# Two attention and two gated-MLP layers on one core: another layout and pacing of the gate/up weight loads, with three smaller edits and new instruction orders

## The chip, the cores and the metric

The kernel runs on one core of one Trainium2 chip. The metric is device time in microseconds (us) for one execution; lower is better. The time of a kernel is the median of its runs, and a profile is one further execution, taken with the hardware profiler.

## What is computed

The input is x, one sequence of 2048 tokens by 448 features in bf16. Four layers follow each other, A, B, A, B, with the same weights for both A and both B, and each adds its result to x:

```python
x = x + _A_ref(_layernorm(x, axis=-1), A_wqkv, A_wo)
x = x + _B_ref(_layernorm(x, axis=-1), B_w_gate, B_w_up, B_w_down)
x = x + _A_ref(_layernorm(x, axis=-1), A_wqkv, A_wo)
x = x + _B_ref(_layernorm(x, axis=-1), B_w_gate, B_w_up, B_w_down)
```

A is attention with 16 heads of 28 features: each token attends to 8 tokens, itself and those 2, 4, ... 14 places before it. B is a gated MLP without a nonlinearity: `(x @ w_gate) * (x @ w_up)`, 1792 wide, then `@ w_down`.

## The kernel before

**Tiling.** Tokens live on partitions in 16 blocks of 128 (`x_sb`); even and odd tokens are stored in separate halves so that the stride of 2 becomes a stride of 1. Each layer runs in chunks of 256 or 512 tokens, and chunks of neighbouring layers interleave in the order of `SEQ` (A00 A01 B10 A02 B11 ...: A, layer 0, chunk 0, and so on). A chunk's rows are normalised on DVE and ACT (L724 to L745) and transposed, in layer 0 by PE with a copy out of PSUM by ACT or DVE (L755 and `ft`, L761), in later layers by a DMA transpose from SP (L748). An A chunk then makes queries and keys (`qk_chunk`, copies at L846) and values (`v_group`), scores (L958), exponentials (L965), masks (L975), the weighted sum (L995), normalisation, and the output product (`y_blocks`). A B chunk (`b_chunk`) has 14 gate/up units of 128 of the 1792 columns. Each unit is seven pairs of matmuls, gate and up side by side: a matmul here uses 64 of PE's 128 rows, so two that use different row halves run at once (helper `pair`, recorded as L489). ACT copies gate out (L1086), DVE multiplies by up (L1089), and the down products follow (L489, and L1101 at the end).

**Weights.** `WGU` holds gate and up for `b_chunk`. Before the change, partitions 0 to 63 hold gate and 64 to 127 hold up, for seven slabs k of 64 weight rows. Eight transfers fill it, one for each quarter of the columns of each matrix, each into 64 partitions with rows of 448 columns (896 bytes); a gate/up unit waits only for the quarters up to its own columns. The four `wo` transfers and the four `WD` transfers come after them, each `WD` transfer only when the one before has landed. The query/key weights arrive in `stage` in four row groups c (they take the space of `hT`), and are spread out into `WQK` by eight copies at L664: for each c one copy of all queries and one of all keys. Small constants go to a DRAM scratch tensor (`vones`), from which DMA transposes later bring part of the values (`vt_load`, L866) after copies out of `qk` (L855).

**Order.** Nothing is ordered by the chip alone. `Sched` collects operations and numbers them as they are added. `ORD` lists, for each of PE, ACT, DVE, POOL and SP, the numbers in the order in which that engine issues them. The estimates in the code (`lat`, `LINE_T` and others) only decide which PSUM banks are handed out and were used to find the lists. In `emit` each operation first waits for the semaphores of all that it depends on, and what follows on the same engine waits behind it. So a DMA on SP that waits for an earlier landing holds up every later DMA of SP. In SP's list of before, numbers 0 to 13 are the head loads, 78 is `vones`, 79 to 86 are gate/up, 87 to 90 `wo`, 91 to 93 the first three `WD`, and then come 291 and 293, the two DMA transposes that the first gate/up chunk (layer 1, chunk 0, 256 tokens) needs.

**Head loads.** SP and ACT issue the loads of x and of the query, key and value weights in the first microseconds. All of x is in five more transfers after the first block; chunk ("x", -1, 4) is the one that brings blocks 4 to 7, ("x", -1, 8) and ("x", -1, 12) the next ones.

Of the kernel before, what the change touches and what calls it, by code (L numbers as in the profile page):

```python
# [4 lines left out]
ACT = mybir.ActivationFunctionType  # L5
# [43 lines left out]
VONES_L = 13300.0  # L49
GUL = (14800.0, 1150.0)  # L50
WOL = 24300.0
# [12 lines left out]
}  # L64
SEQ = "A00 A01 B10 A02 B11 A03 A04 B12 A20 B13 A21 B14 B30 A22 B31 A23 B32 B33 B34".split()

# [1165 lines left out]
```

## Time and profile before

| | before |
|---|---|
| median of 3 runs | 391.69 us (390.35 to 392.07) |
| profiled execution, its own time | 392.11 us |
| its span, first to last instruction | 390.4 us |
| PE busy | 381.7 us, 98% of the span |
| PE weight loads busy | 217.5 us, 56% |
| DVE busy | 281.6 us, 72% |
| ACT busy | 192.7 us, 49% |
| POOL busy | 9.8 us, 3% |
| DMA | 22.49 MB in 56608 packets |
| mean granted TensorE clock | 0.996 |

The span is the time from the first to the last instruction of the program; the execution's own time is 1.7 us longer. A busy PE is not a PE at its peak: matmuls overlap, and a busy stretch may hold a slower clock. The granted clock is the share of full speed that the chip allows TensorE. A line number such as L489 can be that of a helper that makes many instructions, so groups are told apart by tiles as well: `ps<-xnTb,WGU` are gate/up matmuls, `ps<-xnTa,WQK` are queries and keys. The part "idle before" of a group names what ended the engine's waiting; "issue" means that the engine waited for nothing that the profile shows.

### The profile page before, as it was taken

How to read it: one execution, taken by the hardware profiler on the slowest of the kernel's cores; microseconds unless marked ns; L12 is line 12 of the kernel's file. 1: busy time of each engine (PE TensorE's matmuls, PEld its weight loads, DVE VectorE, ACT ScalarE, POOL GpSimd, SP SyncE). 2: the span in 40 equal slices, each digit the busy share in tenths (PEclk: the TensorE clock that was granted, in tenths of full speed). 3: DMA queues.
4: the chain of work that ended last, by engine and by line, in shares of the span. 5: the costliest groups of instructions: out<-in, count | busy, mean ns of one | idle time of the engine just before them, and what ended most of it. 6: DMA issues, size and time to landing. Idle time of an engine off the chain costs nothing.

```text
span 390.4 us, 14264 instructions
## 1 busy us (share of the span) xinstructions
PE 381.7 (98%) x6356; PEld 217.5 (56%) x6356; DVE 281.6 (72%) x609; ACT 192.7 (49%) x380; POOL 9.8 (3%) x41
## 2 busy tenths in 40 slices
PE   7979999999999999999999999999999999999997
PEld 3545558654454545544556678544555555555875
DVE  6967899898988578495667978667687688355423
ACT  4876897563724754065662436453354553033310
POOL 7020000000000000000000000000000000000000
PEclk9989999999999999999999999999999999999999
DMA  8994131900342001420402134130107002304002
GB/s 272 248 205 110 33 69 25 136 11 2 57 79 29 13 14 27 86 44 2 59 17 30 29 63 84 31 55 0 26 5 93 12 0 44 77 2 107 2 25 84
DMA packets 56608, 22.49 MB, mean 58 GB/s; under 512 B 44948, under 2 KB 56548, under 8 KB 56548
## 3 DMA queue, kind: packets, MB, share of 16 engines
q1 hardware_dynamic: 56116, 21.07, 28.0%
q8 instruction: 50, 0.82, 0.9%
q10 hardware_dynamic: 432, 0.52, 0.4%
q14 instruction: 10, 0.08, 0.1%
HBM read 8.54 MB, written 2.71 MB: 29 GB/s over the span
## 4 chain that ended last, share of the span: by engine, by line
PE 94%; DVE 2%; DMA 1%; ACT 1%; issue 1%; ACTq 0%; DVEq 0%
PE ps L489 86%; PE ps L958 3%; PE ps L995 2%; PE ps L492 1%; PE ps L1101 1%; DMA hT<-in_A_wqkv_dram 1%; ACT qk L846 0%; PE ps L755 0%; DVE xn_sb L745 0%; DVE oT L1033 0%; DVE qk L846 0%; DVE hT L1089 0%; ACT R_sb L1021 0%; DVE v_sb L938 0%; ACT O_sb L1006 0%
## 5 line engine op out<-in xcount | busy, mean ns | idle before, releaser
L489 PE MATMUL ps<-xnTb,WGU 64*128 64x512 bf16 (+1 forms) x1938 | 177.0, 333 | 0.0
L489 PEld LDWEIGHTS ps<-xnTb,WGU 64*128 64x128 bf16 x1938 | 97.1, 94 | 68.5 <-issue 1.2
L1086 ACT ACTIVATE g_sb<-ps 128x512 bf16<-128x512 f32 (+1 forms) x140 | 68.9, 510 | 106.3 <-PE ps L489 96.7
L1089 DVE TENSOR_TENSOR hT<-g_sb,ps 128x512 bf16<-128x512 bf16 (+1 forms) x140 | 77.1, 574 | 44.1 <-ACT g_sb L1086 39.4
L489 PE MATMUL ps<-WD,hT 64*128 64x448 bf16 x820 | 84.2, 349 | 0.8 <-DVE hT L1089 0.8
L489 PEld LDWEIGHTS ps<-WD,hT 64*128 64x128 bf16 x820 | 41.0, 94 | 34.1 <-issue 1.1
L489 PE MATMUL ps<-xnTa,WQK 64*128 64x512 bf16 (+1 forms) x500 | 53.6, 359 | 1.1 <-issue 0.7
L1050 DVE TENSOR_TENSOR x_sb<-x_sb,ps 128x448 bf16<-128x448 bf16 x62 | 36.8, 614 | 23.8 <-PE ps L489 23.8
L965 ACT ACTIVATE E_sb<-ps 128x1024 bf16<-128x1024 f32 (+1 forms) x36 | 33.7, 980 | 14.7 <-PE ps L958 14.3
L724 DVE BATCH_NORM_STATS2 st<-x_sb 128x6 f32<-128x448 bf16 x64 | 38.5, 615 | 1.5 <-DMA x_sb<-in_A_x_dram 1.3
L489 PEld LDWEIGHTS ps<-xnTa,WQK 64*128 64x128 bf16 x500 | 23.8, 96 | 24.5 <-issue 1.7
L745 DVE TENSOR_SCALAR xn_sb<-x_sb,mv,rstd 128x896 bf16<-128x896 bf16 (+1 forms) x64 | 36.0, 579 | 1.2 <-ACT rstd L729 1.0
L1021 ACT ACTIVATE R_sb<-R_sb 128x480 f32<-128x480 f32 (+1 forms) x34 | 20.1, 601 | 25.4 <-DVE R_sb L1020 25.3
L975 DVE TENSOR_TENSOR E_sb<-E_sb,MK 128x1024 bf16<-128x1024 bf16 (+2 forms) x40 | 23.9, 611 | 10.9 <-ACT E_sb L965 10.4
L846 ACT ACTIVATE qk<-ps 128x1024 bf16<-128x1024 f32 (+1 forms) x25 | 22.5, 918 | 17.3 <-PE ps L489 17.1
L489 PE MATMUL ps<-wo_g,oT 64*128 64x448 bf16 x252 | 29.1, 350 | 0.1
L1020 DVE STREAM_SHUFFLE R_sb<-O_sb 128x480 f32<-128x480 f32 (+1 forms) x34 | 22.9, 692 | 0.0
L1033 DVE TENSOR_TENSOR oT<-O_sb,R_sb 128x480 bf16<-128x480 f32 (+3 forms) x36 | 22.1, 625 | 0.9 <-ACT R_sb L1022 0.7
L489 PE MATMUL ps<-WV,xnTa 64*128 64x336 bf16 (+3 forms) x248 | 22.4, 304 | 0.1
L1022 ACT ACTIVATE R_sb<-R_sb 128x480 f32<-128x480 f32 (+1 forms) x34 | 19.9, 601 | 0.2
L489 PEld LDWEIGHTS ps<-wo_g,oT 64*128 64x128 bf16 x252 | 12.3, 94 | 11.0 <-DVE oT L1033 0.5
L846 DVE CAST qk<-ps 128x1024 bf16<-128x1024 f32 (+1 forms) x11 | 12.4, 1123 | 6.6 <-PE ps L489 6.6
(59 smaller groups left out, 192.5 us busy)
## 6 DMA issues: line engine op xcount, KB each, us to landing
out_dram<-x_sb SPq DMA_DIRECT2D x15, 112.0 KB, 1.8
WGU<-in_B_w_gate_dram SPq DMA_DIRECT2D x4, 392.0 KB, 8.8
WGU<-in_B_w_up_dram SPq DMA_DIRECT2D x4, 392.0 KB, 9.6
x_sb<-in_A_x_dram SPq DMA_DIRECT2D x3, 448.0 KB, 5.9
WD<-in_B_w_down_dram SPq DMA_DIRECT2D x2, 448.0 KB, 3.7
WD<-in_B_w_down_dram SPq DMA_DIRECT2D x2, 336.0 KB, 3.9
vt<-qk SPq DMA_DIRECT2D x42, 16.0 KB
xnTb<-xn_sb SPq DMA_TRANSPOSE x32, 3.1
```

The source lines that it names most:

```text
L489: return lambda E: E.matmul(out(), lhs(), rhs(), start=start, stop=stop)
L724: sc.add("dve", one(lambda E, B=B: E.bn_stats(st6[:, B, :], x_sb[:, B, :]), ("bn", li, B)), 525.0, deps=[("x", li - 1, B)] + ([("xn", li - ...
L745: sc.add("dve", one(lambda E, B=B, dst=dst, src=src: E.tensor_scalar(dst, src, mv[:, B, 0:1], rstd[:, B:B + 1], ALU.subtract, ALU.mult), ( ...
L846: return E.activation(dst, src, ACT.Copy) if hasattr(E, "activation") else E.tensor_copy(dst, src)
L965: return E.activation(E_sb[:, slot, 2 * hp:2 * hp + 2, 0:w], ps[:, b0:b0 + 2, 0:w], ACT.Exp, scale=SCALE)
L975: return E.tensor_tensor(e, e, m, ALU.mult)
L1020: sc.add("dve", one(lambda E: E.stream_shuffle(R_sb[:, rs, 0:w], O_sb[:, os_, 0:w], [DH] * 32), ("Rs", li, qb)), dve_est(w) + 100.0, deps= ...
L1021: sc.add("act", one(lambda E: E.activation(R_sb[:, rs, 0:w], R_sb[:, rs, 0:w], ACT.Ln), ("Rl", li, qb)), act_est(w, False), deps=[("Rs", l ...
L1033: return E.tensor_tensor(oT[:, :, a % HALF:a % HALF + z - a], O[:, :, a - tok:z - tok], R_sb[:, rs, 0:w].rearrange("p (h n) -> p h n", h=4 ...
L1050: sc.add("dve", one(lambda E: E.tensor_tensor(x_sb[:, B, :], x_sb[:, B, :], ps[:, bk[w], 0:D], ALU.add), ("x", li, B)), dve_est(D), deps=[ ...
L1086: sc.add("act", one(lambda E, gs=gs, bk=bk: E.activation(g_sb[:, gs, 0:nt], ps[:, bk[0], 0:nt], ACT.Copy), ("G", li, j, fc)), act_est(nt), ...
L1089: sc.add("dve", one(lambda E, gs=gs, bk=bk, fc=fc: E.tensor_tensor(hT[:, fc, hs, 0:nt], g_sb[:, gs, 0:nt], ps[:, bk[1], 0:nt], ALU.mult), ...
```

## The change

- **Gate/up layout and loads.** For gate, slab k keeps its 64 weight rows, but the first half of the columns (896) goes to partitions 0 to 63 and the second half to 64 to 127. For up, partitions 0 to 63 take the second half of the columns of slab k, and partitions 64 to 127 the first half of the columns of slab k+1 (of slab 0 for the last). So for each unit gate and up still lie in different partition halves: in units 0 to 6 gate is in the lower and up in the upper half, in units 7 to 13 the other way round, and the matmul pairs are written accordingly. There are 15 transfers in place of 8: seven for gate, six for up, and two of 64 partitions for up's remainder. Thirteen of them have 128 destination partitions, rows of 896 columns (1792 bytes), and a source pattern of three dimensions, `[2, 64, 896]`.
- **Waits.** A unit waits for all 15 transfers, not for the quarters up to its own.
- **Pacing.** `link` adds a transfer to a chain: it waits until the third-last one before it has landed. The chain begins with three loads of x; the 15 gate/up transfers, `vones` and the four `WD` transfers follow. The `wo` transfers now come before all of them.
- **Query/key copies.** Each of the eight copies at L664 takes half of the heads, of queries and keys together. In layer 0's first two chunks the units c = 0 and 1 wait for the first halves only.
- **Transposes.** In layer 0's first chunk the copy out of PSUM is made in two halves, which may go to different engines.
- **Orders.** All five lists in `ORD` are new. The numbering moves: 78 to 81 are `wo`, 82 to 96 gate/up, 97 `vones`, 98 to 101 `WD`, and most later numbers are higher by 9. SP's list begins 0, 1, 4 to 13, 78 to 98 in one run, then 583 (one copy out of `qk`), 302 and 300 (the two DMA transposes for the first gate/up chunk, formerly 293 and 291), then 509 and further copies.

```diff
-VONES_L = 13300.0
-GUL = (14800.0, 1150.0)
-WOL = 24300.0
+GUL = 2900.0
+DEPTH = 3
+WOL = 14000.0
...
-                src = stage[:, 2 * D * c + D * w:2 * D * c + D * (w + 1)].rearrange("p (h e) -> p h e", e=DH)
-                dst = WQK[:, c, w, :].rearrange("p (h e) -> p h e", e=32)[:, :, 0:DH]
+                src = stage[:, 2 * D * c:2 * D * (c + 1)].rearrange("p (w h e) -> p w h e", w=2, e=DH)[:, :, 8 * w:8 * w + 8, :]
+                dst = WQK[:, c, :, 256 * w:256 * w + 256].rearrange("p w (h e) -> p w h e", e=32)[:, :, :, 0:DH]
...
-    head_dma("sp", ones_dst, ones_src, ("vones",), "d_one", VONES_L, deps=["c_ones"])
-    for n in range(4):
-        f0, f1 = F // 4 * n, F // 4 * (n + 1)
-        for w, W_ in enumerate((B_w_gate, B_w_up)):
-            head_dma("sp", WGU[64 * w:64 * w + 64, :, f0:f1], W_[:, f0:f1].rearrange("(k p) f -> p k f", p=64), (("wg", "wu")[w], n), f"d_w{'gu'[w]}{n}", GUL[0] + GUL[1] * (2 * n + w))
...
-    prev = ("wo", 3)
+    chain = [("x", -1, 4), ("x", -1, 8), ("x", -1, 12)]
+
+    def link(dst, src, key, sem, lat, deps=()):
+        plain_dma("sp", dst, src, key, sem, deps=[chain[-DEPTH], *deps], lat=lat)
+        chain.append(key)
+
+    for w, W_ in enumerate((B_w_gate, B_w_up)):
+        for k in range(7):
+            v = W_[64 * k:64 * k + 64, :]
+            r = v.ap[0][0]
+            dst = WGU[:, k, w * F // 2:(w + 1) * F // 2]
+            if w == 0 or k < 6:
+                src = bass.AP(tensor=v.tensor, offset=v.offset + w * F // 2, ap=[[F // 2 if w == 0 else 64 * r - F // 2, 2], [r, 64], [1, F // 2]])
+                link(dst, src, (("wg", "wu")[w], k), f"d_w{'gu'[w]}{k}", GUL)
+            else:
+                link(dst[0:64], v[:, F // 2:F], ("wu", 6), "d_wu6", GUL)
+                link(dst[64:128], W_[0:64, 0:F // 2], ("wu", 7), "d_wu7", GUL)
+    link(ones_dst, ones_src, ("vones",), "d_one", WDL, ["c_ones"])
     for n in range(4):
         f0, f1 = (0, 4, 7, 11, 14)[n:n + 2]
-        plain_dma("sp", WD[:, f0:f1, :], B_w_down[128 * f0:128 * f1, :].rearrange("(c p) e -> p c e", p=128), ("wd", n), f"d_wd{n}", deps=[prev], lat=WDL)
-        prev = ("wd", n)
+        link(WD[:, f0:f1, :], B_w_down[128 * f0:128 * f1, :].rearrange("(c p) e -> p c e", p=128), ("wd", n), f"d_wd{n}", WDL)
...
-            return dict(bk=bk, out=out, lhs=lhs, rhs=rhs, n=n, kind="QKps", deps=WQK0 if (li, j) in NOPW else WQKR, keys=(("Kps", li, j, c), ("Qps", li, j, c)), c=c)
+            return dict(bk=bk, out=out, lhs=lhs, rhs=rhs, n=n, kind="QKps", deps=WQK0 if (li, j) in NOPW and c > 1 else WQK0[::2] if (li, j) in NOPW else WQKR, keys=(("Kps", li, j, c), ("Qps", li, j, c)), c=c)
...
-            return dict(bk=acq, out=out, n=nt, deps=[(w, n) for w in ("wg", "wu") for n in range((128 * fc + 127) // (F // 4) + 1)],
+            return dict(bk=acq, out=out, n=nt, deps=[(w, k) for w in ("wg", "wu") for k in range(7 + (w == "wu"))], row=(64 * r, 64 - 64 * r), col=(col, F // 2 + col),
                         keys=(("Gps", li, j, fc), ("Ups", li, j, fc)), fc=fc)
```

More of the change, by code (lines that the diff above doesn't have):

```diff
@@ L137 @@
     LINE = 256
-    LINE_T = ((75000.0, 4300.0), (24000.0, 5000.0), (11000.0, 6500.0), (-1.0, 5000.0))
+    LINE_T = ((75000.0, 4300.0), (24000.0, 4900.0), (11000.0, 5600.0), (-1.0, 5000.0))
     def __init__(self):
@@ L564, in build @@
     sem_names += [f"d_x{i}" for i in range(NCH)] + ["d_stg0", "d_stg1", "d_stg2", "d_stg3", "d_wv", "d_out", "d_out2"]
-    sem_names += ["d_x0h", "d_x0b"] + [f"d_wo{j}" for j in range(4)] + [f"d_w{w}{n}" for w in "gu" for n in range(4)] + [f"d_wd{n}" for n in range(4)]
+    sem_names += ["d_x0h", "d_x0b"] + [f"d_wo{j}" for j in range(4)] + [f"d_w{w}{n}" for w in "gu" for n in range(8)] + [f"d_wd{n}" for n in range(4)]
     sem_names += [f"d_t{li}_{j}" for li in range(4) for j in range(len(CH[li]))]
@@ L604, in build @@
     load_stage("act", 0, 3650.0)
-    load_stage("act", 2, 4600.0)
-    load_stage("sp", 1, 5300.0)
+    load_stage("act", 2, 5650.0)
+    load_stage("sp", 1, 5850.0)
     load_stage("sp", 3, 6450.0)
@@ L757, in ln_chunk, with ft @@
                 sc.add("pe", ins, 4 * 29.3, deps=[("xn", li, B), "c_id"], mode=MAIN, acquire=bk, prio=prio)
-                def ft(E, c0=c0, bk=bk):
-                    src = ps[:, bk[0]:bk[0] + 2, :].bitcast(bf)[:, :, 0:256].rearrange("p h (c n) -> p c h n", c=4)
-                    dst = X[:, :, c0:c0 + 128].rearrange("p c (h n) -> p c h n", h=2)
-                    return E.activation(dst, src, ACT.Copy) if hasattr(E, "activation") else E.tensor_copy(dst, src)
-                sc.add(("act", "dve"), one(ft, ("T", li, B)), {"act": act_est(512), "dve": dve_est(512)}, deps=[("Tps", li, B)] + war, release=[(bk, 0), (bk, 1)], prio=prio)
+                parts = ((0, 1), (1, 2)) if (li, j) == (0, 0) else ((0, 2),)
+                for a, z in parts:
+                    def ft(E, c0=c0, bk=bk, a=a, z=z):
+                        src = ps[:, bk[a]:bk[a] + z - a, :].bitcast(bf)[:, :, 0:256].rearrange("p h (c n) -> p c h n", c=4)
+                        dst = X[:, :, c0 + 64 * a:c0 + 64 * z].rearrange("p c (h n) -> p c h n", h=z - a)
+                        return E.activation(dst, src, ACT.Copy) if hasattr(E, "activation") else E.tensor_copy(dst, src)
+                    n = 256 * (z - a)
+                    sc.add(("act", "dve"), one(ft, ("T", li, B) if z == 2 else ("Ta", li, B)), {"act": act_est(n), "dve": dve_est(n)}, deps=[("Tps", li, B)] + war, release=[(bk, i) for i in range(a, z)], prio=prio)
     SLOTS = [((0, 0, 0), (1, 0, 64)), ((0, 1, 0), (1, 2, 64)), ((0, 3, 0), (1, 3, 64)),
@@ L817, in qk_chunk @@
         n = c1 - c0
-        tdeps = [("T", li, B) for B in range(c0 // 128, c1 // 128)]
+        tdeps = [("T", li, B) for B in range(c0 // 128, c1 // 128)] + ([("Ta", 0, 0), ("Ta", 0, 1)] if (li, j) == (0, 0) else [])
         war = []
@@ L882, in v_group @@
                 blocks.add(B)
-        tdeps = [("T", li, B) for B in sorted(blocks)] + [p for _, p in slots if p is not None]
+        tdeps = [("T", li, B) for B in sorted(blocks)] + [("Ta", 0, B) for B in sorted(blocks) if li == 0 and B < 2] + [p for _, p in slots if p is not None]
         plain = li == 0 and qbs[0] < PAIR_PLAIN[PAIRED]
@@ L1068, in unit @@
         def unit(fc):
+            r, col = divmod(128 * fc, F // 2)
             acq = Banks(2, kind=1)
@@ L1077, in b_chunk @@
             u = us[m]
-            steps = [pair([(lambda u=u, w=w: u["out"](w), lambda u=u, w=w, k=k: WGU[64 * w:64 * w + 64, k, 128 * u["fc"]:128 * u["fc"] + 128],
-                            lambda w=w, k=k: X[64 * w:64 * w + 64, k, c0:c0 + nt], k == 0, k == 6, 64 * w, u["keys"][w] if k == 6 else None) for w in range(2)]) for k in range(7)]
+            steps = [pair([(lambda u=u, w=w: u["out"](w), lambda u=u, w=w, k=k: WGU[u["row"][w]:u["row"][w] + 64, (k - w * (u["row"][w] > 0)) % 7, u["col"][w]:u["col"][w] + 128],
+                            lambda u=u, w=w, k=k: X[u["row"][w]:u["row"][w] + 64, k, c0:c0 + nt], k == 0, k == 6, u["row"][w], u["keys"][w] if k == 6 else None)
+                           for w in ((0, 1) if u["row"][0] == 0 else (1, 0))]) for k in range(7)]
             sc.add("pe", [i for st, _ in steps for i in st], 7 * pe_cols(nt), deps=u["deps"] + tdeps, mode=MAIN, prio=prio, acquire=u["bk"], alt=alt_of([st for _, st in steps]),
```

10 rows, old and new, of the table ORD are left out of this document.

## The prediction

> **What bounds the kernel now.** I read the page's busy times and its chain of waits first, then PE's timeline for holes, then windows of 2 us for the granted clock, then the DMA view of chosen stretches.
>
> ```profile
> span 390.4 us, 14264 instructions
> ...
> PE 381.7 (98%) x6356; PEld 217.5 (56%) x6356; DVE 281.6 (72%) x609; ACT 192.7 (49%) x380; POOL 9.8 (3%) x41
> ...
> PE 94%; DVE 2%; DMA 1%; ACT 1%; issue 1%; ACTq 0%; DVEq 0%
> ...
> L489 PE MATMUL ps<-xnTb,WGU 64*128 64x512 bf16 (+1 forms) x1938 | 177.0, 333 | 0.0
> ```
>
> PE is busy for 381.7 of 390.4 us and carries 94% of the chain that ends last. The gate/up matmuls, the largest group, wait for nothing (0.0 idle). So only two things can move the time much: the 8.7 us in which PE does nothing, and a new wait on PE's path. Where is PE idle early on, and what was it doing?
>
> ```profile
> 8.25 2.47 PE L489 MATMUL ps<-xnTa,WQK 64*128 64x256 bf16 x42 [0.31 <-DVE st L724]
> ...
> 24.24 0.23 PE L958 MATMUL ps<-qk 28*64 28x64 bf16 x5 [1.42 <-issue]
> ...
> 32.55 0.29 PE L489 MATMUL ps<-xnTa,WQK 64*128 64x256 bf16 x2 [0.71 <-issue]
> ...
> 56.60 3.66 PE L489 MATMUL ps<-xnTb,WGU 64*128 64x256 bf16 x64
> ```
>
> Two holes, 1.42 and 0.71 us, have no releaser: PE waited for nothing that the profile shows. The last row is the one that matters below: the first gate/up matmul runs at 56.60 us, so the weights have until then to land. The windows (length, then PE and PEld, DVE, ACT, POOL busy, granted clock, DMA share, GB/s):
>
> ```profile
> 22.00:24.00 2.00, 0.66 (x59) 0.59 (x60) 0.94 (x3) 1.08 (x4) 1.83 (x8) 1.00 1.13 206
> 24.00:26.00 2.00, 1.76 (x61) 0.97 (x62) 0.96 (x2) 1.13 (x2) 0.00 (x0) 0.78 1.14 211
> 26.00:28.00 2.00, 2.00 (x18) 0.82 (x14) 1.83 (x5) 1.26 (x3) 0.00 (x0) 0.50 1.11 202
> 28.00:30.00 2.00, 2.00 (x36) 1.64 (x32) 0.71 (x3) 1.97 (x6) 0.00 (x0) 0.87 0.79 152
> ```
>
> After the hole the granted clock is 0.78, 0.50 and 0.87 for three windows, which loses 2 x (0.22 + 0.50 + 0.13) = 1.7 us of PE. All of it falls where the DMA engines are full (share 1.1) but move only some 205 GB/s. That is the eight gate/up loads, each into 64 partitions. Loads into 128 partitions ran faster; the rows are those of the stretches 4 to 10 us and 14 to 28 us:
>
> ```profile
> DMA packets 2170, 2.09 MB, mean 348 GB/s; under 512 B 113, under 2 KB 2170, under 8 KB 2170
> ```
>
> ```profile
> DMA packets 3348, 2.91 MB, mean 208 GB/s; under 512 B 124, under 2 KB 3346, under 8 KB 3346
> ```
>
> **The change part by part.**
>
> *Matmuls.* Each gate/up unit keeps 14 matmuls of the same shapes on the same row halves; the order within a pair turns for units 7 to 13. Nothing.
>
> *The gate/up loads.* All hangs on how many of the 16 DMA engines carry a load. Every transfer ends with small packets, and they can be counted. In the stretch 34 to 37.1 us there is one `WD` load (336 KB, 128 partitions); in 132.5 to 137 us there are seven copies out of `qk`, of four rows each:
>
> ```profile
> DMA packets 400, 0.34 MB, mean 111 GB/s; under 512 B 16, under 2 KB 400, under 8 KB 400
> ```
>
> ```profile
> DMA packets 141, 0.13 MB, mean 29 GB/s; under 512 B 28, under 2 KB 140, under 8 KB 140
> ...
> vt<-qk SPq DMA_DIRECT2D x7, 16.0 KB
> ```
>
> 384 packets of 896 B make the 336 KB, and 16 small ones are left over: one an engine. The seven copies have 28, four each, for patterns whose outermost dimension is 4. So I read that a transfer is dealt out along its outermost dimension. Thirteen of the new loads have 128 rows as destination but `[2, 64, 896]` as source. Do the 128 decide or the 2? One transfer of before has sides that differ, `vones`: 32 partitions on one side, 8 outermost on the other. The list of DMAs gives no time to landing for it, just as for the transfers of 28 and 4 rows, while those of 128 rows have one:
>
> ```profile
> WV<-in_A_wqkv_dram SPq DMA_DIRECT2D x2, 224.0 KB, 6.0
> ...
> wo_g<-in_A_wo_dram SPq DMA_DIRECT2D x4, 98.0 KB
> ...
> vt<-ones SPq DMA_DIRECT2D x1, 128.0 KB
> ```
>
> 32 alone would share out evenly on 16, so this points to both sides having to divide, and the smaller one deciding. I take two engines for the thirteen loads.
>
> The Trainium skill has the same as a rule ("DMA: Bandwidth & Descriptors", section "Why a DMA increments its semaphore by 16 and not by 1"): a transfer uses the largest number of engines up to 16 that divides the outermost dimension above 1 of both patterns. By that rule the thirteen loads get two engines, which is the sum below; by the same page's advice to load 128 partitions at once ("Rules for kernel authors") it would be the first rival. The counts of 16 and 4 agree with the first; no row here shows a source of 2.
>
> What does a load cost on two engines? Each moves 64 rows of 1792 B, 114,688 B. Queue 10 in the first 10 us carried only ACT's two query/key loads, whose rows are also 1792 B; with it the GB/s row of that stretch:
>
> ```profile
> GB/s 0 0 0 0 0 0 0 90 190 211 344 369 373 369 344 362 323 301 337 294 315 312 355 330 333 294 287 337 362 384 373 380 383 376 387 366 387 366 380 380
> ...
> q10 hardware_dynamic: 288, 0.46, 12.7%
> ```
>
> 0.46 MB took 12.7% of 16 engines for 10 us, 20.3 us: 22.6 GB/s an engine, or 5.07 us a load. The best slice, 387 GB/s over 16, is 24.2 GB/s, or 4.74 us. In that first stretch the queue shared its engines, so I take 4.9 us, and keep both ends. Three under way keep two engines fed without a gap, so thirteen loads last 63.7 us.
>
> *When they begin and what they hold up.* SP's timeline of before, and the landing of its last head load:
>
> ```profile
> 6.14 1.86 SPq L579 DMA_DIRECT2D hT<-in_A_wqkv_dram  x2
> 8.04 0.91 SPq L579 DMA_DIRECT2D vt<-ones  x1
> ...
> 49.96 2.68 SPq L748 DMA_TRANSPOSE xnTb<-xn_sb  x2
> 52.97 5.14 SPq L855 DMA_DIRECT2D vt<-qk  x14
> 59.16 1.13 SPq L866 DMA_TRANSPOSE v_sb<-vt  x1
> ```
>
> ```profile
> xnTb<-xn_sb SPq DMA_TRANSPOSE x32, 3.1
> ...
> hT<-in_A_wqkv_dram SPq DMA_DIRECT2D x2, 56.0 KB, 5.4
> ```
>
> The last head load is issued by 8.0 us and lands near 12.5. The four `wo` loads (392 KB) now follow, 1.2 us at 348 GB/s: the chain has its engines from 13.7 us, and its two-engine part ends at 13.7 + 63.7 = 77.4. SP issues in order: `vones` waits for the last up load but two, the first `WD` for the next, and both stand ahead of one copy out of `qk` and of the two DMA transposes that the first gate/up chunk needs. Before, those were issued at 49.96. Now they come after 77.4 + 1 (landing) + 1.7 (issues: 0.91 for `vones`, the `WD` load and the copy at 5.14/14 = 0.37 each). From the first issue to the second landing are 1.3 + 3.1 = 4.4 us. So gate/up starts at 77.4 + 1 + 1.7 + 4.4 = 84.5 in place of 56.6: **27.9 us in which PE, whose list goes in order, does nothing.** Then the clock: an idle PE got half clock after the hole at 22 us, and lost 1.7 us. A longer hole should cost that once (bounds 0 and twice, 3.4).
>
> Behind the waits: 21 copies out of `qk` (14 before) and the other three `WD` loads now go ahead of the first `vt_load`. After the transposes' own issues (until 82.8) 23 x 0.37 us put it at 91.3, some 7 us after gate/up's start, against 59.16 - 56.60 = 2.6. The gate/up matmuls of that chunk (14 units) hide that; without them it would cost up to 4 us.
>
> *Earlier edits.* In before the first query/key matmul (8.25) follows ACT's two copies of transposes:
>
> ```profile
> 6.99 1.16 ACT L761 ACTIVATE xnTa<-ps 128x512 bf16<-128x512 bf16 x2 [0.55 <-PE ps L755]
> ```
>
> Halves on ACT and DVE together take about half of that 1.16, and the first units need half of the L664 copies: 0.3 to 0.6 us earlier. It is worth nothing in front of a 28 us wait, and its cover is that wait. The same goes for the holes at 24 and 32 us.
>
> *The new orders.* All of PE's matmuls stay. Past 56.6 us PE has one stretch with holes before its tail:
>
> ```profile
> 70.00:80.00 10.00, 9.20 (x236) 5.60 (x234) 7.64 (x21) 5.27 (x12) 0.00 (x0) 1.00 0.90 96
> 80.00:100.00 20.00, 20.00 (x262) 9.47 (x262) 18.32 (x42) 10.91 (x23) 0.00 (x0) 1.00 0.01 2
> ```
>
> So another order can win 0.8 us there, and lose about as much by holes of its own: from -0.8 to +1; I take 0.
>
> *Sum.* The profiled execution took 392.11 us, 1.7 more than its span and 0.4 above the median. 392.1 + 27.9 + 1.7 = 421.7, less 0.4: **421 us** as a median. Its own range: with 4.74 us a load, start at 13.0, 1.5 us for landing and issues and no clock loss, gate/up starts at 80.5: 415.6. With 5.07, start 14, 3.7 us, 6 us for transposes queued behind `vones` and `WD`, and 3.4 of clock: start 89.6, 428. With the orders' 1 us at each end and some width for the engine rate, 413 to 430.
>
> **The rivals.** PE fetches its instructions by DMA, too; the row for 20 to 25 us, one packet of 16 KB ahead of the hole at 24:
>
> ```profile
> q8 instruction: 1, 0.02, 1.7%
> ```
>
> 1. *The 128 destination rows decide; the loads run on 16 engines.* For it: the counts only show transfers with equal sides; `vones` is read from a missing number. Then 3.2 MB at 348 GB/s are 9 us, or 15 us if three under way can't fill the engines, and all is in by 30, long before 56.6. The DMA queue is never deep, the two holes without a releaser (1.42 + 0.71) go, if a full DMA is what holds up that fetch, and with them the slow clock (1.7); the start gives 0.3 to 0.6. That is 4.3: 387.4, between 385.5 and 389.7. It decides from loads under 3 us each.
> 2. *16 engines, and the gain is lost.* The last 10 us before gate/up:
>
> ```profile
> 50.00:60.00 10.00, 9.77 (x248) 6.45 (x246) 9.09 (x21) 9.10 (x17) 0.00 (x0) 1.00 0.37 71
> ```
>
> DVE and ACT are both at 9.1 of 10 there. A PE that arrives 4 us sooner waits for them instead: 390 to 393.5. Against it: from 22 to 30 both have room (the windows above).
>
> 3. *16 engines, but the chain is slow.*
>
> ```profile
> WGU<-in_B_w_gate_dram SPq DMA_DIRECT2D x4, 392.0 KB, 8.8
> ```
>
> Before, a gate load took 8.8 us from issue to landing. Five rounds of three at 8.8 are 44 us: in by 57, gate/up at 57 + 7 = 64, so 7.4 later: 399. Against it: that 8.8 is mostly queueing.
>
> **How the numbers follow.** Two engines 0.70; rival 1 0.22; rival 2 0.04; rival 3 0.04. Two engines' own range, 413 to 430, holds about 0.66, so a range for 8 in 10 must reach the other side: 387 to 430 takes in rivals 2 and 3 and the upper half of rival 1. Half a per cent, 2 us, is about what a measurement of this kernel can tell from no change: faster 0.22, same 0.04, slower 0.74.
>
> **What would show it.** Two engines: a DMA share near 2/16 at some 47 GB/s from 15 to 77 us; two small packets a load; PE idle from about 55 to 84; a granted clock of 0.5 behind it; SP's transposes after 77. Rival 1: loads landing within 3 us, no hole at 24 and 32, clock 1.00 throughout, gate/up before 56. I am wrong on the step "smaller side decides" if the DMA view shows over 200 GB/s while the gate/up loads run.

## The result and the profile after

| | before | after |
|---|---|---|
| median | 391.19 us (4 runs, 390.35 to 392.07) | 420.74 us (4 runs, 420.67 to 421.92) |
| ratio to before | | 1.0762, interval 1.0729 to 1.0795 |
| profiled execution, its own time | 392.11 us | 420.71 us |
| its span | 390.4 us | 418.9 us |
| gate/up begins | 56.60 us | 83.64 us |

The changed kernel is 29.55 us slower; 421 was predicted. First its page: the span, TensorE's busy time, the engines' shares of the chain of waits, and the gate/up group.

```profile
span 418.9 us, 14291 instructions
...
PE 381.5 (91%) x6356; PEld 217.7 (52%) x6356; DVE 284.5 (68%) x614; ACT 188.7 (45%) x377; POOL 9.2 (2%) x41
...
PE 80%; DMA 17%; SPq 1%; DVE 1%; ACT 0%; issue 0%
...
L489 PE MATMUL ps<-xnTb,WGU 64*128 64x512 bf16 (+1 forms) x1938 | 177.7, 336 | 31.8 <-DMA xnTb<-xn_sb 31.8
```

The work is what it was (381.7 us busy before, 381.5 now). What is new is one idle time of 31.8 us ahead of a gate/up matmul, and 17% of the chain that is DMA. TensorE's timeline shows where (start, length, operation, idle time ahead of it and its releaser):

```profile
7.75 2.80 PE L489 MATMUL ps<-xnTa,WQK 64*128 64x256 bf16 x48 [0.34 <-ACT xnTa L774]
...
50.88 0.93 PE L489 MATMUL ps<-wo_g,oT 64*128 64x448 bf16 x8
83.64 7.91 PE L489 MATMUL ps<-xnTb,WGU 64*128 64x256 bf16 x112 [31.83 <-DMA xnTb<-xn_sb]
91.47 0.71 PE L972 MATMUL ps<-qk 28*64 28x64 bf16 x64
```

TensorE finishes its attention work at 51.81 us and then does nothing until 83.64. The holes of 1.42 and 0.71 us that before had near 24 and 32 us aren't in this timeline. The releaser named, the DMA transpose, is only the last link; SyncE's timeline has the chain ahead of it:

```profile
10.05 23.79 SPq L579 DMA_DIRECT2D WGU<-in_B_w_gate_dram  x7
38.29 33.90 SPq L579 DMA_DIRECT2D WGU<-in_B_w_up_dram  x8
76.65 0.83 SPq L579 DMA_DIRECT2D vt<-ones  x1
77.54 0.51 SPq L579 DMA_DIRECT2D WD<-in_B_w_down_dram  x1
78.16 0.37 SPq L869 DMA_DIRECT2D vt<-qk  x1
78.58 2.67 SPq L759 DMA_TRANSPOSE xnTb<-xn_sb  x2
...
90.30 6.81 SPq L880 DMA_TRANSPOSE v_sb<-vt  x4
```

The eight issues of up take 33.90 us, each held until the load three before it has landed: some 4.8 us from one to the next. Behind the last of them come `vones`, the first `WD`, one copy, and only then the two transposes that gate/up needs. The windows of 4 us (length, then PE, PEld, DVE, ACT, POOL busy, granted clock, DMA share, GB/s) show how those loads ran, and what the wait did to the clock:

```profile
28.00:32.00 4.00, 4.00 (x132) 2.77 (x104) 3.26 (x10) 3.07 (x6) 0.00 (x0) 1.00 0.15 52
...
56.00:60.00 4.00, 0.00 (x0) 0.00 (x0) 0.00 (x0) 0.00 (x0) 0.00 (x0) 0.53 0.13 48
60.00:64.00 4.00, 0.00 (x0) 0.00 (x0) 0.00 (x0) 0.00 (x0) 0.00 (x0) 0.50 0.13 48
...
84.00:88.00 4.00, 4.00 (x52) 3.42 (x48) 1.21 (x4) 1.73 (x4) 0.00 (x0) 0.63 0.46 120
```

DMA is busy for 0.13 to 0.15 of 16 engines, about two of them, at some 50 GB/s, where before had a share of 1.1 and 205 GB/s. The clock falls to 0.50 some 4 us into the wait and is at 0.63 in the first 4 us of gate/up. The DMA view of the stretch 20 to 60 us counts the small packets; its last row is the queue of these loads (packets, MB, share):

```profile
DMA packets 1093, 2.03 MB, mean 51 GB/s; under 512 B 16, under 2 KB 1085, under 8 KB 1085
...
q1 hardware_dynamic: 1085, 1.92, 13.1%
```

Sixteen small ones belong to the eight loads or so that end in these 40 us: two a load (one for each engine, as the prediction reads them).

### The profile page after: what moved, and what is told of

The parts are those of the page before. It is cut to its first block, busy times and chain, and to the rows that moved or that the text cites. A ratio compares the mean times of both kernels' runs of the same rounds, so it can differ in the third digit from the quotient of the medians.

```text
span 418.9 us, 14291 instructions
## 1 busy us (share of the span) xinstructions
PE 381.5 (91%) x6356; PEld 217.7 (52%) x6356; DVE 284.5 (68%) x614; ACT 188.7 (45%) x377; POOL 9.2 (2%) x41
## 4 chain that ended last, share of the span: by engine, by line
PE 80%; DMA 17%; SPq 1%; DVE 1%; ACT 0%; issue 0%
PE ps L489 73%; DMA WGU<-in_B_w_gate_dram 9%; DMA WGU<-in_B_w_up_dram 7%; PE ps L972 2%; PE ps L1009 2%; PE ps L655 1%; PE ps L1117 1%; PE ps L492 1%; DMA xnTb<-xn_sb 1%; SPq L579 1%; SPq L759 0%; DVE st L735 0%; ACT qk L860 0%; ACT v_sb L952 0%; DVE x_sb L1121 0%
## 5 line engine op out<-in xcount | busy, mean ns | idle before, releaser
L489 PE MATMUL ps<-xnTb,WGU 64*128 64x512 bf16 (+1 forms) x1938 | 177.7, 336 | 31.8 <-DMA xnTb<-xn_sb 31.8
L1105 DVE TENSOR_TENSOR hT<-g_sb,ps 128x512 bf16<-128x512 bf16 (+1 forms) x140 | 77.4, 574 | 67.7 <-ACT g_sb L1102 66.0
L489 PE MATMUL ps<-xnTa,WQK 64*128 64x512 bf16 (+1 forms) x500 | 51.4, 353 | 0.5 <-ACT xnTa L774 0.3
L860 ACT ACTIVATE qk<-ps 128x1024 bf16<-128x1024 f32 (+1 forms) x24 | 21.1, 898 | 15.2 <-PE ps L489 14.9
L738 ACT ACTIVATE lnv<-mv,eps_sb 128x2 f32<-128x2 f32 (+1 forms) x33 | 9.6, 295 | 28.3 <-DVE mv L737 28.1
```

The costliest lines, as they stand in the source:

```text
L489: return lambda E: E.matmul(out(), lhs(), rhs(), start=start, stop=stop)
L860: return E.activation(dst, src, ACT.Copy) if hasattr(E, "activation") else E.tensor_copy(dst, src)
L1105: sc.add("dve", one(lambda E, gs=gs, bk=bk, fc=fc: E.tensor_tensor(hT[:, fc, hs, 0:nt], g_sb[:, gs, 0:nt], ps[:, bk[1], 0:nt], ALU.mult), ...
```

## The experiments

All kernels are the changed one with an edit, except where it is said; each ratio is to the kernel before, run beside it. My theory: thirteen loads run on two engines because their source has an outermost dimension of 2. The rivals: they are slow for another reason (the chain of three; a source that jumps; a load across both partition halves), or the place of the transposes in SyncE's list costs more than the loads.

**1. The same thirteen loads, each as two loads of 64 rows.** Layout, chain and orders stay.

```diff
-   src = bass.AP(tensor=v.tensor, offset=v.offset + w * F // 2, ap=[[F // 2 if w == 0 else 64 * r - F // 2, 2], [r, 64], [1, F // 2]])
-   link(dst, src, (("wg", "wu")[w], k), f"d_w{'gu'[w]}{k}", GUL)
+   up = W_[64 * k + 64 * w:64 * k + 64 * w + 64, :]
+   halves(dst, v[:, w * F // 2:(w + 1) * F // 2], up[:, (1 - w) * F // 2:(2 - w) * F // 2], ...)
```

> Each of the thirteen 128-row loads is issued as two loads of 64 rows (source outermost 64); layout, matmuls, chain and orders stay. Two engines as the cause: the loads spread over 16 engines, are in by about 30 us, gate/up starts near 52 us without a wait, 387 us (386 to 389). Pacing as the cause (three links under way are too few): a link still takes some 14 us, so 421. The new layout or the wait for all fifteen as a cost of its own: slower than 391 with no wait for loads.

Measured: 390.45 us (10 runs, 388.12 to 392.92), ratio 0.9998 (0.9974 to 1.0023). All 29.55 us are back. TensorE's timeline, and then SyncE's:

```profile
51.64 6.29 PE L489 MATMUL ps<-xnTb,WGU 64*128 64x256 bf16 x112
...
65.69 0.38 PE L1013 MATMUL ps<-E_sb,v_sb 64*32 64x64 bf16 x21 [1.67 <-DMA v_sb<-vt]
```

```profile
57.87 7.84 SPq L884 DMA_TRANSPOSE v_sb<-vt  x4
```

The DMA view of 18 to 30 us, in which only these loads and instructions move:

```profile
DMA packets 1331, 1.96 MB, mean 164 GB/s; under 512 B 256, under 2 KB 1328, under 8 KB 1328
```

About 16.7 loads of 114,688 B fit into the loads' 1.92 MB of this, and 256 small packets are some sixteen a load.

SyncE issues `vones`, behind the loads, at 33.04 us in place of 76.65, and gate/up begins at 51.64, right behind the attention work and 4.96 us earlier than before. But the time is that of before, not 387, so that forecast missed. One part of the loss has a row: TensorE waits 1.67 us for the `v_sb<-vt` transposes, which SyncE issues behind all 21 copies out of `qk`.

**2. Without the chain of three.** From the fourth load on, each waits only for the last load of x.

```diff
-   plain_dma("sp", dst, src, key, sem, deps=[chain[-DEPTH], *deps], lat=lat)
+   plain_dma("sp", dst, src, key, sem, deps=[chain[-DEPTH] if len(chain) < 6 or key[0] in ("vones", "wd") else chain[2], *deps], lat=lat)
```

> The thirteen loads stay as they are, but from the fourth on a gate/up load waits only for the last load of x, so all are queued by about 20 us; the scratch constants and the down weights keep their waits. Two engines as the cause: the same bytes go through the same two engines, the last lands near 76 us, 420.7 (418 to 422.5). Pacing as the cause: all in by 30 us, 387 to 391.

Measured: 421.6 us (2 runs), ratio 1.0787 (1.0747 to 1.0827). Gate/up in TensorE's timeline:

```profile
84.27 8.56 PE L489 MATMUL ps<-xnTb,WGU 64*128 64x256 bf16 x112 [31.49 <-DMA xnTb<-xn_sb]
```

And SyncE's issues of up:

```profile
34.63 34.55 SPq L579 DMA_DIRECT2D WGU<-in_B_w_up_dram  x8
```

The loads were not all queued by 20 us, as I had expected: the issues now follow each other without a wait, but last until 69 us. So it isn't shown that many more were under way. Still, the chain no longer holds a load back and the time is no shorter: the chain isn't the cause.

**3. Only the first three gate loads as halves.**

```diff
+   if w == 0 and k < 3:
+       halves(dst, v[:, w * F // 2:(w + 1) * F // 2], up[:, (1 - w) * F // 2:(2 - w) * F // 2], ...)
+       continue
```

> Only the first three gate loads are issued as two loads of 64 rows; ten stay as they were. Two engines as the cause: three times 4.74 us less two-engine work and about 3 us more on all engines, so gate/up starts some 11 us earlier, 409.5 (408 to 412). Pacing as the cause: 421.

Measured: 413.93 us (2 runs), ratio 1.0591 (1.0552 to 1.063): 6.8 us gained, too little for what was expected. SyncE's timeline, then TensorE's:

```profile
68.38 0.82 SPq L579 DMA_DIRECT2D vt<-ones  x1
```

```profile
75.19 9.10 PE L489 MATMUL ps<-xnTb,WGU 64*128 64x256 bf16 x112 [22.97 <-DMA xnTb<-xn_sb]
```

`vones` is held until 68.38 in place of 76.65, 8.3 us less, where three loads at 4.8 are 14.4. The halves need their time too: the first of the ten remaining loads is issued at 16.64, where the changed kernel has its first at 10.05. Then the first 112 gate/up matmuls take 9.10 us in place of 7.91, since the clock stays low for longer. 8.45 earlier at gate/up less 1.2 is 7.2. The direction is as expected, and what I got wrong is the size.

**4. The two transposes ahead of `vones` and `WD`.**

```diff
-"... 96 97 98 583 302 300 509 ..."
+"... 96 583 302 300 97 98 509 ..."
```

> Only SP's order changes: one copy out of qk and the two transposes that the first gate/up chunk needs go ahead of the scratch constants and the first down load. The sum in the prediction puts 1.7 us of issues and 4.4 us of transposes behind the last landing: the transposes then land near 78 us and gate/up starts at 79 to 80, 416.5 (415.5 to 418). If the weights' landing alone set the start, it stays at 420.7.

Measured: 418.62 us (2 runs), ratio 1.071 (1.0668 to 1.0753). TensorE's timeline:

```profile
79.04 7.81 PE L489 MATMUL ps<-xnTb,WGU 64*128 64x256 bf16 x112 [26.11 <-DMA xnTb<-xn_sb]
...
94.61 0.41 PE L1009 MATMUL ps<-E_sb,v_sb 64*32 64x64 bf16 x21 [1.68 <-DMA v_sb<-vt]
```

The window behind that second wait (columns as above):

```profile
96.00:100.00 4.00, 4.00 (x32) 1.94 (x28) 2.43 (x6) 1.58 (x5) 0.00 (x0) 0.59 0.93 125
```

Gate/up begins 4.6 us earlier, as expected, but the time gains only 2.1, and the profiled span 1.4. Of the rest, 1.68 us is the wait of experiment 1, and 1.7 us is lost behind it, where the granted clock is 0.59. SyncE's list is worth some 2 to 5 us of the 29.55.

**5. and 6. Halves whose source counts 2 or 4 outermost.** As experiment 1, but each 64-row source is written as 2 groups of 32 rows (even, odd), or as 4 groups of 16. Its destination stays one block of 64 partitions.

```diff
+   def rows(v):
+       r = v.ap[0][0]
+       return bass.AP(tensor=v.tensor, offset=v.offset, ap=[[r, 2], [2 * r, 32], [1, F // 2]])
```

> As the run with halves, but each 64-row load's source is written as two groups, the even rows and then the odd ones, so that its outermost dimension counts 2, its destination stays one block of 64 partitions and its rows keep one distance within a group (the rows of the gate and up weights stand in another order than the activations, and the output is not the reference's). Theory one, the outermost count sets the number of engines: two engines carry all 26 loads, the transfers need the same 60 us as in the changed kernel, DMA share near 0.15 from 16 to 70 us, gate/up starts near 83, 419 to 422. Theory two, the changed kernel's loads are slow because one load spans both partition halves or because its source jumps by an odd distance: these loads are as quick as the halves, gate/up starts at 51.7, 390.5.

Measured: 422.35 us (2 runs), ratio 1.0805 (1.0768 to 1.0841). One window, and the DMA view of 20 to 60 us:

```profile
28.00:32.00 4.00, 4.00 (x130) 2.74 (x126) 3.27 (x10) 2.56 (x5) 0.00 (x0) 1.00 0.15 52
```

```profile
DMA packets 1112, 2.03 MB, mean 51 GB/s; under 512 B 34, under 2 KB 1104, under 8 KB 1104
```

> As the run with two groups, with each 64-row load's source in four groups of 16 rows (row 0, 4, 8 ..., then row 1, 5, 9 ... and so on; the rows of the gate and up weights stand in another order than the activations, so the output is not the reference's). If the number of engines is the outermost count, four carry the 26 loads: DMA share near 0.25 to 0.30 and 95 to 105 GB/s, 26 x 114,688 bytes in about 30 us from 12, last load in near 43 to 46, before TensorE needs it: gate/up near 51.7 and 390.5 (388 to 393). If any regrouping of the rows leaves two engines, 419 to 422 as with two groups.

Measured: 394.29 us (3 runs), ratio 1.0096 (1.0073 to 1.0119). The same window with four groups and two later ones, the DMA view of 18 to 40 us, and TensorE's timeline:

```profile
28.00:32.00 4.00, 4.00 (x134) 2.85 (x134) 3.26 (x9) 2.92 (x6) 0.00 (x0) 1.00 0.28 101
...
68.00:72.00 4.00, 3.07 (x100) 2.17 (x102) 1.86 (x8) 1.59 (x4) 0.00 (x0) 0.74 0.77 49
72.00:76.00 4.00, 4.00 (x110) 2.28 (x108) 2.75 (x7) 1.63 (x5) 0.00 (x0) 0.83 1.06 157
```

```profile
DMA packets 1243, 2.17 MB, mean 98 GB/s; under 512 B 74, under 2 KB 1237, under 8 KB 1237
```

```profile
54.43 6.29 PE L489 MATMUL ps<-xnTb,WGU 64*128 64x256 bf16 x112 [2.43 <-DMA xnTb<-xn_sb]
...
68.93 0.41 PE L1016 MATMUL ps<-E_sb,v_sb 64*32 64x64 bf16 x21 [2.12 <-DMA v_sb<-vt]
```

This is the run that decides. These loads neither cross the partition halves nor jump to another slab, and with two groups they are as slow as in the changed kernel: share 0.15, 52 GB/s, 34 small packets for about 17 loads, two each. With four groups the rate doubles, to 0.28 and 101 GB/s, with 74 for about 18, four each. So at these two counts the outermost count of the source sets the number of engines, and 64 outermost gave sixteen small packets a load (experiment 1). Four are still a little too few: gate/up waits 2.43 us, where I expected none. SyncE issues `vones` at 46.91 and the transposes at 48.84, in place of 44.90 with the halves. The time is longer by more than that, since the clock falls to 0.74 and 0.83 behind the next wait, of 2.12 us, which loses another 1.7 us.

**7. The layout of before in 64-row loads, with the chain and the new orders.** Gate below, up above, all columns: 14 loads of 64 rows by 3584 B, the last in two.

```diff
+   for k in range(7):
+       for w, W_ in enumerate((B_w_gate, B_w_up)):
+           v, dst = W_[64 * k:64 * k + 64, :], WGU[64 * w:64 * w + 64, k, :]
...
+               link(dst, v, (("wg", "wu")[w], k), f"d_w{'gu'[w]}{k}", GUL)
```

> The layout of before (gate in the lower 64 partitions, up in the upper, all columns), loaded as 14 loads of 64 rows by 3584 bytes (the last one in two), gate and up in turn, with the chain of three and the new orders kept. If the plain 64-row source is what spreads a load over 16 engines, the loads need about as long as the halves did, all are in before 45 us, gate/up starts at 51.7, and the time is that of the run with halves, 390.5 (388 to 393): the new layout by itself is worth nothing then. Rival: a 64-partition load goes at 208 GB/s however it is cut and the chain leaves gaps, so that the last load lands after 50 and gate/up starts later than 52: 392 or more.

Measured: 390.15 us (10 runs, 388.16 to 391.66), ratio 0.9984 (0.996 to 1.0008). Gate/up in its timeline:

```profile
52.69 6.29 PE L489 MATMUL ps<-xnTb,WGU 64*128 64x256 bf16 x112
```

No wait ahead of it, and the time of the halves. The new layout by itself is worth nothing that can be measured.

**8., 9. and 10. Where the holes without a releaser came from.** First the halves without the chain, with the edit of experiment 2 for the halves as well:

```diff
-   ... deps=[chain[-DEPTH]], dma=sem, mode=0, lat=lat)
+   ... deps=[chain[-DEPTH] if len(chain) < 6 else chain[2]], dma=sem, mode=0, lat=lat)
```

> The loads as halves, and from the fourth on without the chain: each waits only for the last load of x. Theory: the two holes in TensorE's stream of before, 1.42 and 0.71 us with no releaser, and its granted clock of 0.50 to 0.87 around 24 us come with a full DMA queue. Then they come back here near 20 to 30 us, and the start of gate/up moves from 51.6 to 53 to 56, time 391 to 394. Rival: they came from before's order of work, and do not come back; gate/up at 51.6 and 390.5 as with the chain.

Measured: 391.89 us (8 runs, 389.81 to 393.41), ratio 1.003 (1.001 to 1.005). Gate/up began at 51.87, and there was no hole near 24 or 32. But this tests nothing, for the queue wasn't full: the DMA share was 0.64 in the window from 20 to 24 us. The median is 1.4 us above that of the halves; six of the eight executions had a mean granted clock of 0.995 or 0.996 (391.81 to 393.41 us), and the two at 1.00, one of them the profiled one, took 389.81 and 390.44. So the 14 long loads of experiment 7 without the chain, by the edit of experiment 2:

> The layout of before in 14 loads of 64 rows by 3584 bytes with the new orders, and from the fourth load on without the chain: each waits only for the last load of x, so that all are issued before 20 us and lie in the queue together. (With the halves the chain could be left out without that: 26 issues of 0.65 us each kept the DMA share at 0.5 to 0.65.) Theory: the holes without a releaser that TensorE had in both profiles of before, 1.3 to 1.5 us near 24 and 0.7 to 1.5 us near 32 us, come with a DMA share over 1. Then the share is over 1 up to about 24 us, the holes are here again, 1 to 3 us in all, gate/up starts at 53.5 to 55.5 in place of 52.7, and the time is 391 to 393. Rival: the holes came from before's order of instructions, the stream has none, and gate/up starts at 52 to 53 with 390.2 as with the chain.

Measured: 390.97 us (10 runs, 389.38 to 392.6), ratio 1.0 (0.9977 to 1.0023). That window, and TensorE's timeline:

```profile
20.00:24.00 4.00, 3.31 (x120) 2.08 (x118) 2.70 (x8) 3.86 (x6) 2.52 (x12) 1.00 1.04 237
```

```profile
29.83 0.22 PE L1006 MATMUL ps<-E_sb,v_sb 64*32 64x64 bf16 x8 [1.29 <-issue]
...
53.68 6.29 PE L489 MATMUL ps<-xnTb,WGU 64*128 64x256 bf16 x112
```

Behind a stretch with a share over 1 one hole of 1.29 us is back, with the new orders, and gate/up begins 0.99 us later than in experiment 7. That fits the theory, but it is one profile, and the hole itself, 28.54 to 29.83, lies where the queue had nearly emptied (share 0.11 from 28 to 30 us). Last, the kernel before a second time:

> The kernel before once more, for a second profile of it (the one that the prediction was worked out from took 392.11 us, above the median of 390.7 of the runs since). If the two holes in TensorE's stream, 1.42 and 0.71 us near 24 and 32 us, and the granted clock of 0.50 to 0.87 behind the first belong to each execution, they are here again and gate/up starts near 56.6. If they are an accident of that execution, one or both are gone, gate/up starts 1 to 3.5 us earlier and the span is 388 to 389; the gain of the halves, 4 to 5 us by the profiles, is then smaller by as much.

Measured: one execution, 392.25 us, beside a median of 390.92 for ten others. Its TensorE timeline:

```profile
24.29 0.23 PE L958 MATMUL ps<-qk 28*64 28x64 bf16 x5 [1.26 <-issue]
...
32.05 0.29 PE L489 MATMUL ps<-xnTa,WQK 64*128 64x256 bf16 x2 [1.46 <-issue]
```

Both holes are here again, and gate/up begins at 56.10: in both profiles they belong to the kernel. The low clock behind the first hole isn't (1.00 from 8 to 68 us), so that comes in some executions only. What sits in the holes stays open. The prediction's row has one packet of 16 KB of instructions ahead of the hole at 24, where the queue is full, and such a packet could wait in it; but ahead of the second hole the queue is nearly empty (share 0.06 from 30 to 32 us in the first profile, 0.02 in the second), as in experiment 9. No run here moves such a packet by itself.

**11. SyncE's list mended, with the halves.** The fourteen copies that the first value transposes need, then those transposes, in the order in which TensorE wants them; the last seven copies behind them.

```diff
-"... 96 97 98 583 302 300 509 581 365 582 580 512 507 368 367 510 99 364 366 513 579 369 363 584 100 508 101 578 511 378 518 517 377 434 ..."
+"... 96 97 98 302 300 365 368 367 364 366 369 363 99 509 512 507 510 513 508 511 518 517 100 101 378 377 583 581 582 580 579 584 578 434 ..."
```

> The loads as halves, and SyncE's order after the last gate/up load changed: first the seven copies out of qk that the first v_sb<-vt transposes need, then the next seven, then the two transposes that the first output product waits for (blocks 9 and 10), the next two, and only then the last seven copies. Theory: in the run with halves the five microseconds that the head gained were given back in part at one wait of 1.67 us for v_sb<-vt, because 20 copies stood ahead of the first transposes (issued at 57.87). With 14 copies ahead they are issued near 54.5, land before 62, and TensorE reaches its output product at 64.0 without a wait: span near 386, median 388.8 (387.5 to 390), ratio to before 0.995. Rival: the wait only moves, to the fourth transpose or to the first WD product, and the time stays at 390.5.

Measured: 389.92 us (12 runs, 389.05 to 391.9), ratio 0.9985 (0.9968 to 1.0002). SyncE issues the first transposes at 57.19, with 14 copies ahead of them, and TensorE's timeline reads:

```profile
8.62 2.80 PE L489 MATMUL ps<-xnTa,WQK 64*128 64x256 bf16 x48 [0.34 <-ACT xnTa L778]
...
52.53 6.28 PE L489 MATMUL ps<-xnTb,WGU 64*128 64x256 bf16 x112
...
64.96 0.27 PE L1013 MATMUL ps<-E_sb,v_sb 64*32 64x64 bf16 x21
```

The wait is gone. The profiled execution took 389.05 us, 3.1 less than that of before, but the medians differ by only 0.75 us, and the interval reaches past no change. So this version isn't shown to beat before.

**12. The query/key copies of before, with the halves.** The two copies of each row group again one of queries and one of keys, and the first product waits for all eight.

```diff
-   src = stage[:, 2 * D * c:2 * D * (c + 1)].rearrange("p (w h e) -> p w h e", w=2, e=DH)[:, :, 8 * w:8 * w + 8, :]
+   src = stage[:, 2 * D * c + D * w:2 * D * c + D * (w + 1)].rearrange("p (h e) -> p h e", e=DH)
...
-   deps=WQK0 if (li, j) in NOPW and c > 1 else WQK0[::2] if (li, j) in NOPW else WQKR
+   deps=WQK0 if (li, j) in NOPW else WQKR
```

> The loads as halves, and the query/key copies of before (by query and key, and not by columns), with the wait of the first product for all eight of them. The prediction put the start of the first product 0.3 to 0.6 us earlier by the copies by columns, and this at nothing for the end while a wait stood behind it. With the halves no such wait stands behind: the first product near 8.25 in place of 7.75, gate/up near 52.1 in place of 51.6, time 390.5 to 391. Rival: the first product waits for its activations anyway, and nothing moves.

Measured: 391.04 us (8 runs, 389.49 to 393.5), ratio 1.0014 (0.9993 to 1.0035). The first product in TensorE's timeline:

```profile
8.40 2.80 PE L489 MATMUL ps<-xnTa,WQK 64*128 64x256 bf16 x48 [1.31 <-DVE mv L741]
```

TensorE now waits 1.31 us ahead of it, against 0.34 in the changed kernel and in experiment 11, and gate/up begins at 52.43, against 51.64 with the halves alone. So under the new orders the edit is worth some 1.0 us at the first product by the waits, and 0.8 at gate/up in these two profiles; the forecast was 0.3 to 0.6. In the median it is 0.6 us, within what the runs scatter by. A start alone doesn't tell: in experiment 11 the first product began at 8.62 and gate/up at 52.53 with the new copies, behind earlier matmuls that took longer.

## Why the prediction was right, step by step

- **"The smaller side decides", two engines: right**, and shown by experiments 5, 6 and 1, with two, four and sixteen small packets a load for counts of 2, 4 and 64, and 52 and 101 GB/s for 2 and 4. The rule cited from the Trainium skill ("DMA: Bandwidth & Descriptors", section "Why a DMA increments its semaphore by 16 and not by 1") is borne out by these runs. The same page of the Trainium skill, in "Rules for kernel authors", calls two transfers to disjoint partition halves not worth the trouble; here they gave back all 29.55 us, because the one transfer of 128 partitions was written with a 2 outermost.
- **4.9 us a load: right.** The loads' queue moved 1.92 MB in 40 us, 48 GB/s, or 4.8 us for 229,376 B. The two-engine loads were through at 76.65, forecast as 77.4 + 1.
- **+1.7 and +4.4 us behind the last load: about right.** The transposes were issued 1.9 us after the release of `vones`, and gate/up came 5.1 after that, 0.7 more than forecast. It began at 83.64, forecast as 84.5.
- **"27.9 us in which PE does nothing": the shift was right, the wait wasn't.** The start moved by 27.0 us, but TensorE idled for 31.8. The difference is the head's gain: holes and low clock gone and an earlier first product made the attention work end 4.8 us earlier, and all of that went into the wait, as "worth nothing" said.
- **1.7 us of slow clock: right, with luck in the size.** The first 112 gate/up matmuls took 7.91 us in place of 6.28, so 1.6. Waits of 31.5, 26.1 and 23.0 us (experiments 2, 4 and 3) cost 2.3, 1.5 and 2.8 by the same count.
- **New orders 0, `vt_load` hidden: right in this kernel.** From the end of those 112 matmuls' stretch (91.47 here, 62.81 before) to the end of the span are 327.4 us here and 327.6 before. `v_sb<-vt` was issued at 90.30 (forecast 91.3), and TensorE didn't wait for it. Where gate/up begins earlier in relation to SyncE's list, as with the halves, the same list costs 1.67 us.
- **Sum:** 27.0 + 1.6 - 0.2 is 28.5 between the spans (before rounding); 29.6 was forecast. That 421 lies within 0.3 us of the median owes something to luck: the sum for the profiled execution, 421.7, was 1.0 too high, and the 0.4 taken off for the median has no counterpart in the changed kernel (420.71 profiled, 420.74 median).
- **Rival 1's price was wrong.** Sixteen engines are not 387.4 but 390: experiments 1, 7 and 11 have all that rival 1 asked for (loads in by 37 us, no hole, clock 1.00, gate/up near 52) and end at 389.9 to 390.5. One part is the wait of 1.67 us. Another is the base: "0.4 above the median" held for three runs, but the profiled executions of before took 392.11 and 392.25 where its median over ten to 29 runs is 390.6 to 390.9, while those of the halves and of the mended list lay 0.9 to 1.0 below their own medians. So a gain of 2.7 to 3.1 us between profiled executions is 0.2 to 0.75 between medians. For the halves a part of this is on record, in the mean granted clock of each execution: six at 0.999 or 1.00, among them the profiled one, have a median of 389.69 us, and four at 0.996 one of 391.61. In experiment 7 the two medians are 389.32 and 391.25, five executions each. In before, run beside the halves, they are 390.48 (eight) and 390.87 (five). So a gain of about 0.8 us at full clock is lost again where the clock falls; in the profile with four groups, 0.996 as well, this came behind the wait of 2.12 us. Why before's second profiled execution, at 1.00, took 392.25 stays open.
- **Rivals 2 and 3.** Rival 2 named 390 to 393.5, where these kernels end, but not its mechanism: in experiments 1 and 7 TensorE's only wait over 0.6 us between the first product and 68 us is for `v_sb<-vt`, not for DVE or ACT. Rival 3's 8.8 us a load isn't seen: with the halves a load lands about 3 us after its issue (DMA view of 14 to 35 us).

## What to carry to other kernels

A load whose source is written as "half, row, column" has the half outermost, and here it was dealt to two DMA engines, with a destination of 64 partitions as with one of 128; written as two loads of 64 rows each it went to sixteen. When a profile shows a DMA share near 2/16 for as long as a group of loads runs, look at the outermost count before looking at pacing. And when a change makes one stage earlier, look at what an in-order issuing engine has queued for the next stage: here a gain of 5 us at gate/up was given back, in part to such a wait and in some executions, it seems, to the clock.

## What else the runs showed of the hardware

- 64-partition loads moved 237 GB/s with rows of 3584 B and a full queue (experiment 9), where before moved 202 to 211 with rows of 896 B. The loads also differ in that each of before takes all seven slabs, so the row length isn't shown to be the cause; but the prediction put all of that lower rate down to the 64 partitions, and that can't be the whole of it.
- Half clock began 2 to 5 us into each long wait (4.5 in the changed kernel, 2.0 in experiment 4, 5.0 in experiment 5). What the matmuls behind it lost, 1.5 to 2.8 us, didn't go with the length of the wait. Short waits brought it at times: behind 1.68 us (experiment 4) and 2.12 us (the four groups) the clock fell, behind 2.43 us (the four groups) and 1.67 us (experiment 1) it didn't. What decides isn't shown.
- A DMA share over 1 until 24 us or later went with holes of 0.7 to 1.5 us in TensorE's stream without a releaser, in three profiles of three. The profiles whose share stayed at 0.75 or less from 16 to 48 us had none over 0.4 us. Only the hole near 24 in before lies inside the full stretch; the others come behind it, where the share is 0.02 to 0.11.
